# First batch's K loaded as fp32 on another queue, and half of the second batch's query transposes moved to TensorE

## The chip, the cores and the metric

The kernel runs on one core of one Trainium2 chip. The metric is device time in microseconds (us) of one execution. Traces are of single executions; where one execution differs from another by chance, the text says so.

## The reference

Linformer attention followed by a gated feed-forward layer. K and V are projected along the sequence by E and F (1024 to 64), then each query attends to 64 projected keys:

```python
k_proj = np.einsum('ks,bhsd->bhkd', E, k)        # E, F: 64 x 1024
v_proj = np.einsum('ks,bhsd->bhkd', F, v)
scores = scale * np.matmul(q, k_proj.transpose(0, 1, 3, 2))
attn = softmax(scores);  out = np.matmul(attn, v_proj)   # 8 batches, 8 heads, 1024 x 64
...
gate = 1.0 / (1.0 + np.exp(-(x @ w_gate)))       # x: 8192 x 512, d_ff 1536
return (gate * (x @ w_val)) @ w_out
```

## The kernel before

The feed-forward layer of one batch runs on TensorE while the attention of the next batch is slipped in between its matmuls. The first batch has nothing to hide behind: its K, Q and V must arrive, be projected and attended before the first feed-forward matmul. q, k, v and the weights are fp32 in memory and are cast to bf16 by the load, which the POOL queue issues. E and F go uncast on the SyncE queue. `busy(n)` issues n matmuls that compute nothing of use.

```python
def start_loads():
    for src, rows, n in ((E, slice(0, 64), "E"), (F, slice(64, 128), "F")):
        add("SP", lambda e, ...: e.dma_start(EF[rows, :], src[:, :]), ...)
    load_k(0)                     # POOL queue, casts to bf16
    ...                           # iota constants on POOL
    load_q_half(0, 0); load_v(0)
    ...
    load_w(0); load_w(1); load_q_half(0, 1); load_w(2); load_w(3)

def project_consts():             # 8 fp32 transposes of E and F, copied to EFT as bf16
    ...

start_loads()
constants()
project_consts()
busy(56)
bk = whole.next()
project(0, 0, [bk, bk], 0)        # K of batch 0: 16 bf16 matmuls of 256 columns
keep_k(bk, 0); turn_k(whole)
qt, sc, den, bc, xo = half_unit(0, whole)
qt(0); qt(1); sc(0); sc(1); den() # query transposes, scores, denominators
project(1, 1, bks, 0)             # V of batch 0
...                               # then the feed-forward loop; in it, for batch 1:
put(3, lambda: transpose_q(1))    # four DMA transposes of the queries
```

The softmax here doesn't subtract the row's maximum and nothing guards it: scores larger than these inputs give would overflow.

## Time and profile before

| | kernel before |
|---|---|
| time, median of 3 (range) | 580.94 us (580.69 to 581.57) |
| span of the profiled execution | 579.7 us |
| TensorE busy | 559.1 us, 96% |
| K, first half of Q, V of batch 0 landed | 12.65, 15.3, 20.4 us |
| unbroken feed-forward matmuls from | 25.81 us |
| from there to the end | 553.9 us |

### The profile page before, as it was taken

The numbers are of one execution on the slowest core, as the hardware profiler recorded it, in microseconds if no ns is written. First come the engines' busy times: TensorE is split into PE (matmuls) and PEld (weight loads), VectorE is DVE, ScalarE is ACT, GpSimd is POOL, SyncE is SP. The second block draws the span as 40 slices with busy tenths as digits, with TensorE's granted clock in tenths as the row PEclk, the third lists the DMA queues.
The fourth block names the chain that finished last, engine by engine and source line by source line (L and its number), as shares of the span: only waits on it lengthen the run. The fifth ranks groups of instructions, "written<-read, shape, count | busy, mean of one in ns | idle before, by whom it ended". The sixth has DMA issues, their size and how long they took to land.

```text
span 579.7 us, 7813 instructions
## 1 busy us (share of the span) xinstructions
PE 559.1 (96%) x3150; PEld 253.9 (44%) x3206; DVE 253.3 (44%) x393; ACT 201.0 (35%) x371; POOL 30.3 (5%) x43
## 2 busy tenths in 40 slices
PE   5799899999999999999999999999999999999997
PEld 4444334444454444444444444444445444444443
DVE  2355265345633636236442365434463363633332
ACT  1454541444233351343323433243423335222220
POOL 8100010100100000000100001000000000000000
PEclk9999999999999999999999999999999999999999
DMA  9999998963943049511586027650411001000012
GB/s 153 201 206 193 139 165 155 183 133 75 162 97 75 31 109 181 91 38 48 101 162 110 19 73 117 139 92 36 74 54 38 35 21 37 37 36 20 36 37 90
DMA packets 70756, 55.04 MB, mean 95 GB/s; under 512 B 31168, under 2 KB 62400, under 8 KB 70720
## 3 DMA queue, kind: packets, MB, share of 16 engines
q0 software_dynamic: 31776, 29.89, 33.5%
q1 hardware_dynamic: 38944, 24.65, 16.5%
q8 instruction: 25, 0.41, 0.3%
q14 instruction: 11, 0.09, 0.1%
HBM read 60.29 MB, written 16.78 MB: 133 GB/s over the span
## 4 chain that ended last, share of the span: by engine, by line
PE 85%; DMA 10%; POOL 2%; DVE 1%; issue 1%; SPq 0%; POOLq 0%; DVEq 0%
PE pF L216 77%; PE pA L216 8%; DMA Qb<-in_q_dram 5%; DMA qT<-Qb 5%; DVE rden L685 1%; POOL wV L234 1%; POOL wG L234 1%; POOL KV L234 0%; POOL Qb L234 0%; SPq L622 0%; DVE rhl L695 0%; DVE ost L826 0%; DVE hT L799 0%; DVE rhi L693 0%; POOL pat_i L298 0%
## 5 line engine op out<-in xcount | busy, mean ns | idle before, releaser
L799 DVE SCALAR_TENSOR_TENSOR hT<-sig,pF 128x512 bf16<-128x512 f32 x192 | 131.2, 686 | 210.0 <-PE pF L216 140.0
L220 ACT ACTIVATE sig<-pF 128x512 f32<-128x512 f32 x192 | 115.3, 601 | 273.6 <-PE pF L216 266.1
L216 PE MATMUL pF<-xT,wG 128*128 128x512 bf16 x749 | 195.4, 380 | 2.2 <-issue 1.4
L216 PE MATMUL pF<-xT,wV 128*128 128x512 bf16 x748 | 195.1, 379 | 1.9 <-DVE xT L604 0.9
L216 PE MATMUL pF<-wO,hT 128*128 128x512 bf16 x704 | 163.4, 379 | 1.6 <-issue 1.1
L216 PEld LDWEIGHTS pF<-xT,wV 128*128 128x128 bf16 x768 | 75.1, 98 | 90.8 <-issue 0.6
L216 PEld LDWEIGHTS pF<-xT,wG 128*128 128x128 bf16 x768 | 71.2, 98 | 94.0 <-issue 14.5
L216 PEld LDWEIGHTS pF<-wO,hT 128*128 128x128 bf16 x720 | 68.7, 98 | 86.4 <-issue 5.8
L826 DVE TENSOR_SCALAR ost<-pF 128x512 f32<-128x512 f32 x60 | 41.5, 691 | 89.1 <-PE pF L216 89.1
L220 ACT ACTIVATE rb<-pA 128x512 f32<-128x512 f32 x62 | 32.2, 606 | 26.6 <-PE pA L216 26.6
L220 ACT ACTIVATE eT<-pA 128x512 bf16<-128x512 f32 x63 | 32.8, 603 | 11.3 <-PE pA L216 11.3
L733 DVE TENSOR_TENSOR xT<-pA,rb 128x512 bf16<-128x512 f32 x56 | 34.6, 680 | 0.0
L685 DVE RECIPROCAL rden<-pA 128x128 f32<-128x128 f32 x28 | 23.7, 908 | 0.0
L234 POOL DMA_DIRECT2D KV<-in_k_dram x8 | 7.2, 904 | 265.7 <-PE pF L216 208.6
L216 PE MATMUL pA<-KV,EFT 128*64 128x256 bf16 x240 | 14.6, 274 | 0.9 <-DMA KV<-in_k_dram 0.9
L220 ACT ACTIVATE kp<-pA 128x256 bf16<-128x256 f32 x8 | 3.1, 383 | 35.9 <-PE pA L216 35.9
L216 PEld LDWEIGHTS pA<-KV,EFT 128*64 128x64 bf16 x240 | 12.5, 110 | 4.1 <-issue 3.0
L216 PE MATMUL pA<-qT,kpD 64*64 64x512 bf16 (+1 forms) x140 | 10.6, 367 | 2.1 <-DMA qT<-Qb 1.8
L234 POOL DMA_DIRECT2D KV<-in_v_dram x8 | 7.1, 885 | 80.2 <-PE pA L216 80.2
L220 ACT ACTIVATE vpD<-pA 64x256 bf16<-64x256 f32 x28 | 10.5, 375 | 0.5
L216 PE MATMUL pA<-wO,hT 128*128 128x512 bf16 x47 | 10.5, 379 | 0.1
L216 PE MATMUL pA<-eT,vpD 64*64 64x512 bf16 (+1 forms) x136 | 10.4, 370 | 0.0
(72 smaller groups left out, 113.1 us busy)
## 6 DMA issues: line engine op xcount, KB each, us to landing
out_dram<-ost SPq DMA_DIRECT2D x64, 256.0 KB, 2.0
KV<-in_k_dram POOLq DMA_DIRECT2D x8, 1024.0 KB, 10.1
KV<-in_v_dram POOLq DMA_DIRECT2D x8, 1024.0 KB, 13.2
Qb<-in_q_dram POOLq DMA_DIRECT2D x7, 1024.0 KB, 15.0
wO<-in_moe_w_out_dram POOLq DMA_DIRECT2D x1, 1536.0 KB, 50.2
Qb<-in_q_dram POOLq DMA_DIRECT2D x2, 512.0 KB, 16.5
wG<-in_moe_w_gate_dram POOLq DMA_DIRECT2D x2, 512.0 KB, 23.8
wV<-in_moe_w_val_dram POOLq DMA_DIRECT2D x2, 512.0 KB, 25.6
```

The costliest lines, as they stand in the source:

```text
L216: return add("PE", lambda e: e.matmul(o, lhsT, rhs, **kw), r=r, x=[("bank", b)])
L220: return add("ACT", lambda e: e.activation(o, i, func, scale=scale), r=r, w=w, x=x)
L234: add("POOL", lambda e: e.dma_start(o, i), r=r, w=w, dma=sem)
L685: lambda e, cc=cc: e.reciprocal(rden[:, cc], bank[bk][:, cc]),
L733: lambda e, r=r, g=g, n=n, bk=bks[g]: e.tensor_tensor(xT[s][:, r, :, 256 * g : 256 * g + 256], bank[bk][:, :].rearrange("p (f c) -> p f c" ...
L799: lambda e: e.scalar_tensor_tensor(hT[blk % 2][:, m, :], sg[:, :], 1.0, bank[pv][:, :], ALU.add, ALU.mult,),
L826: lambda e: e.tensor_scalar(o[:, :], bank[pb][:, :], 0.5, None, op0=ALU.mult),
```

## The change

The intent: get the first batch's K to TensorE sooner by not casting it and by using queues that are free at the start, and remove the wait for the last DMA transpose of the second batch's queries.

```diff
         for src, rows, n in ((E, ...), (F, ...)):
-                    "SP",
+                    "ACT",
                     lambda e, ...: e.dma_start(EF[rows, :], src[:, :]),
-            load_k(0)
+            for n in range(2):                        # K of batch 0, fp32, four heads each
+                add("SP", lambda e, n=n: e.dma_start(KF[n],
+                        k[0].rearrange("h (p t) d -> p h (t d)", t=NT)[:, 4*n : 4*n+4, :]), ...)
 ...
+        load_q_half(0, 0, r=["ident"]); load_v(0)     # now after all iotas
 ...
+                act(ETf[:, 4*g : 4*g+4, :], ... )     # fp32 copy of the turned E
 ...
         project_consts()
-        busy(56)
+        busy(6)
-        project(0, 0, [bk, bk], 0)
+        for n in range(2):                            # 2 x 16 fp32 matmuls of 128 columns
+            for t in range(NT):
+                for h in range(2):
+                    mm(bk, bank[bk][64*h : 64*h+64, P*n : P*n+P], ETf[:, t, :], kv4[:, h, t, :, :], ...)
 ...
-                put(3, lambda: transpose_q(1))
+                put(3, lambda: transpose_q(1, (2, 3)))
+                put(12, lambda: turn_q(1, 0))         # 8 TensorE transposes, one copy on VectorE
+                put(13, lambda: turn_q(1, 1))
```

The two fp32 halves of K lie in buffers that are not used yet (the second batch's turned queries, and the second buffer of attention outputs). The tile names in the profile therefore read `qT` and `xT`.

More of the change, by code (lines that the diff above doesn't have):

```diff
@@ L166, in bass_linformer_attn__then__ffn_glu_sigmoid_kernel @@
         EFT = sbuf("EFT", [P, NT, P], BF16)
+        ETf = sbuf("ETf", [P, NT, 64], FP32)
         Qb = [sbuf(f"Qb{i}", [P, H, S // P * DH], BF16) for i in range(2)]
@@ L265, in load_q, with load_q_half @@
             )
-        def load_q_half(b, hf):
+        def load_q_half(b, hf, r=()):
             s, cc = b % 2, slice(256 * hf, 256 * hf + 256)
@@ L273, in load_q_half @@
                 f"Q{s}{hf}",
+                r=r,
             )
@@ L281, in load_w @@
             load(wV[:, :, c], wv_v[:, :, c], [("wV", j)], f"wV{j}")
+        KA = qT[1][:, :, :].rearrange("p h c -> p (h c)").bitcast(FP32)
+        KB = xT[1][:, :, :, :].rearrange("p i f c -> p (i f c)").bitcast(FP32)
+        KF = [x.rearrange("p (h c) -> p h c", h=4) for x in (KA, KB)]
+        KFK = [[("qT", 1, r) for r in range(NR)], [("xT", 1, i, f, g) for i in range(NI) for f in range(2) for g in range(2)]]
         def start_loads():
@@ L291, in start_loads @@
                 )
-            load_k(0)
+            for n in range(2):
+                add(
+                    "SP",
+                    lambda e, n=n: e.dma_start(
+                        KF[n],
+                        k[0].rearrange("h (p t) d -> p h (t d)", t=NT)[:, 4 * n : 4 * n + 4, :],
+                    ),
+                    w=KFK[n],
+                    dma=f"KF{n}",
+                )
             pool(lambda e: e.iota(col_i[:, :], [[1, P]], channel_multiplier=0), w=["col_i"])
             pool(lambda e: e.iota(row_i[:, :], [[1, 1]], channel_multiplier=1), w=["row_i"])
-            load_q_half(0, 0)
-            load_v(0)
             pool(
@@ L309, in start_loads, with loads_q_v_w @@
             )
+        def loads_q_v_w():
+            load_q_half(0, 0, r=["ident"])
+            load_v(0)
             load_w(0)
@@ L407, in project_consts @@
             ev = EF[:, :].rearrange("k (p t) -> k t p", t=NT)
+            bs = []
             for g in range(2):
@@ L418, in project_consts @@
                     )
+                act(
+                    ETf[:, 4 * g : 4 * g + 4, :],
+                    bank[b][:, :].rearrange("p (t c) -> p t c", t=4)[:, :, 0:64],
+                    [],
+                    [("ETf", g)],
+                    b=b,
+                )
+                bs.append(b)
+            for g, b in enumerate(bs):
                 act(
@@ L615, in half_unit, with turn_q, transpose_q @@
             return qt, sc, den, bc, xo
-        def transpose_q(b):
+        def turn_q(b, r):
+            s, bk = b % 2, att.next()
+            ob = bank[bk][:, :].bitcast(BF16)
+            for h in range(2):
+                for t in range(4):
+                    c = 4 * h + t
+                    mm(
+                        bk,
+                        ob[:, c * P : (c + 1) * P],
+                        Qb[s][:, 2 * r + h, t * P : (t + 1) * P],
+                        ident[:, :],
+                        [("Q", s, 0), ("Q", s, 1), "ident"],
+                        tr=True,
+                    )
+            dve(
+                lambda e: e.tensor_copy(
+                    qT[s][:, 2 * r : 2 * r + 2, :].rearrange("p h c -> p (h c)"), ob[:, :]
+                ),
+                [],
+                [("qT", s, r)],
+                b=bk,
+            )
+        def transpose_q(b, rs=range(NR)):
             s = b % 2
-            for r in range(NR):
+            for r in rs:
                 add(
@@ L841, in bass_linformer_attn__then__ffn_glu_sigmoid_kernel @@
         constants()
+        loads_q_v_w()
         project_consts()
-        busy(56)
+        busy(6)
         bk = whole.next()
-        project(0, 0, [bk, bk], 0)
+        for n in range(2):
+            kv4 = KF[n].rearrange("p (r h) (t d) -> p h t r d", h=2, t=NT)
+            for t in range(NT):
+                for h in range(2):
+                    mm(
+                        bk,
+                        bank[bk][64 * h : 64 * h + 64, P * n : P * n + P],
+                        ETf[:, t, :],
+                        kv4[:, h, t, :, :],
+                        [("ETf", t // 4)] + KFK[n],
+                        start=(t == 0),
+                        stop=(t == NT - 1),
+                        tp=(0, 64 * h),
+                    )
         keep_k(bk, 0)
```

## The prediction

> **What bounds the kernel now.** I read the page first, then the timeline of the first 75 us, then the waits of TensorE, and the DMA issues of the first 16 us one by one. The page settles the large picture:
>
> ```profile
> span 579.7 us, 7813 instructions
> PE 559.1 (96%) x3150; PEld 253.9 (44%) x3206; DVE 253.3 (44%) x393; ACT 201.0 (35%) x371; POOL 30.3 (5%) x43
> PE   5799899999999999999999999999999999999997
> ```
>
> TensorE is busy nearly everywhere; only the first two slices (29 us) are thin. The waits of TensorE over the whole span say the same: beyond 2.5 us of issue gaps spread over the run, every wait of note is in the start, except one of 1.8 us:
>
> ```profile
> PE pA L216 <- DMA EF<-in_F_dram: 5.6, 1, 5.6
> PE pA L216 <- DMA qT<-Qb: 1.8, 1, 1.8
> PE pA L216 <- DMA KV<-in_k_dram: 0.9, 1, 0.9
> PE pF L216 <- DVE xT L604: 0.9, 1, 0.9
> PE pF L216 <- DMA Qb<-in_q_dram: 0.7, 1, 0.7
> PE pF L216 <- DMA KV<-in_v_dram: 0.6, 1, 0.6
> ```
>
> The columns are total, count and longest. So the change can only win in two places: the time before the dense feed-forward matmuls begin, and that one wait. TensorE's timeline shows both; columns are start, length, instruction group, and in brackets the idle time before it:
>
> ```profile
> 5.59 1.94 PE L216 MATMUL pA<-identf,EF 128*128 128x128 f32 x8 [5.59 <-DMA EF<-in_F_dram]
> 7.33 4.45 PE L216 MATMUL pF<-ident 128*128 128x128 bf16 x56
> 12.71 1.06 PE L216 MATMUL pA<-KV,EFT 128*64 128x256 bf16 x16 [0.94 <-DMA KV<-in_k_dram]
> 15.37 1.07 PE L216 MATMUL pF<-ident,Qb 128*128 128x128 bf16 x16 [0.68 <-DMA Qb<-in_q_dram]
> 20.48 1.06 PE L216 MATMUL pF<-KV,EFT 128*64 128x256 bf16 x16 [0.58 <-DMA KV<-in_v_dram]
> 25.30 0.38 PE L216 MATMUL pF<-xT,wV 128*128 128x512 bf16 x1 [0.86 <-DVE xT L604]
> ...
> 69.80 0.41 PE L216 MATMUL pA<-qT,kpD 64*64 64x512 bf16 x4
> 72.00 0.41 PE L216 MATMUL pA<-qT,kpD 64*64 64x512 bf16 x4 [1.79 <-DMA qT<-Qb]
> ```
>
> K, the first half of Q, and V each arrive a little after TensorE could take them; the 56 filler matmuls merely fill the wait for K. The dense part begins at 25.3 us. The last two lines are the second batch's scores, which wait for the last of four DMA transposes. The traffic behind these waits, by stage (the two numbers at the end are the DMA share and GB/s written to their destination):
>
> ```profile
> 2.00:4.00 2.00, 0.00 (x0) 0.00 (x0) 1.33 (x11) 0.02 (x1) 1.91 (x5) 1.00 0.80 227
> 4.00:10.00 6.00, 4.41 (x36) 4.37 (x37) 2.75 (x11) 1.19 (x2) 6.00 (x11) 1.00 0.99 142
> 10.00:25.00 15.00, 10.68 (x174) 7.62 (x172) 4.82 (x9) 6.80 (x13) 5.62 (x7) 1.00 1.36 201
> ```
>
> The casting loads write bf16, so 201 GB/s written is 402 GB/s read. From 4 to 10 us they run at only 142 (284 read), although DMA is never idle: some 0.35 MB, or 1.8 us at the later rate, is lost there.
>
> **What the Trainium skill says.** "DMA: Bandwidth & Descriptors", section "Issuing engines are not separate DMA queues": loads begun by the scalar, sync and gpsimd engines run on the same 16 DMA engines and interleave, so another queue saves only issue time. The trace before cannot refute it, but its two phases do differ: E and F from the SyncE queue reach 227 GB/s written in 2 to 4 us, the casting queue alone 142 after that. The section "SWDGE vs HWDGE vs iDMA" of the same page says that a cast needs the gpsimd path, which is why K must go as fp32 here. "FP8 and Floating Point Precision", section "TensorE Precision Notes": a true fp32 matmul takes four passes. The trace before has fp32 only as transposes (217 ns apart), so this is untested. "TensorE: Matmul & The Clock Gate", section "What's actually happening": TensorE runs at half rate until about 3.4 us of activity. The trace agrees: 12 of the filler matmuls begin in the microsecond from 8 us and 22 in that from 10 us, though the clock row of the page shows full speed.
>
> **The change part by part.**
>
> *K as fp32 on SyncE, E and F on ScalarE.* Removed: one casting load, issued at 1.25 and landed 11.4 us later, at 12.65. Added: two plain loads of 1 MB each, issued about 0.74 and 1.4 (where E and F stood before), with E and F beside them on ScalarE's queue. E and F landed 3.8 and 4.1 us after issue; sharing with K, I give them until about 6. Bytes read are unchanged (E and F 0.5 MB, K 2.1, half of Q 1.05, V 2.1 MB), bytes written for K double. At 400 GB/s E, F and K alone take 6.5 us from about 2.3, so 8.8; with the first Q and V packets in between I estimate 8 to 8.5 us for the first half of K and 11 (10 to 12) for the second.
>
> *Projection of K in fp32.* Before, 16 matmuls of 256 columns took 1.06 us: 53 ns apart, half of what 256 columns take alone (about 110 ns), so the two column halves run as pairs. After, 32 matmuls of 128 columns in four passes: a pair is 4 x 55 = 220 ns, eight pairs for a half of K 1.76 us, plus 0.16 tail, 1.9 us. The first half's share lies in the wait for the second half (even at the half rate 3.5 us, it would end near 12). On the path: 1.9 instead of 1.06.
>
> So: K landed 11.0, projected 12.95; then as before 0.5 us to the copy's end, 0.5 to the turned K, then the Q transposes (Q should be there by 12.5 instead of 15.3), which now begin at about 13.9 instead of 15.37. Scores follow at 15.4 instead of 16.86. That is 1.45 us sooner, and the chain to the V projection moves with it to 19.0, provided V lands by then.
>
> *V and everything behind it in the DMA stream.* V landed at 20.4. If the slow phase from 4 to 10 us is filled by K at the full rate, up to 2.5 us is won; if fp32 K is written at about 315 GB/s, it costs 6.7 us where its bf16 form needed 5.2 at 201, and about 1 us is left. I take 1.7: V at 18.7, just in time. The same shift applies to every later load, and they are tight: the third weight chunk landed at 33.5 for a matmul at 34.8, V of the second batch at 56.5 for 57.2, the output weights at 65.4 for 67.1. A start of the dense part sooner by more than the stream's shift plus these slacks would meet new waits. The gain at the start: 1.4 us.
>
> *Small parts.* Two more copies on ScalarE (128x256 took 0.38 us each) before the fp32 K matmuls lie within the wait for K. 50 fillers fewer cost nothing, if TensorE is otherwise busy enough to reach full rate.
>
> *Half of the transposes on TensorE.* Added: 16 transposes of 128x128; the same 16 for the second half of the first batch occupy 0.89 us of the dense part (30.86 to 31.75). Two copies of 0.69 us on VectorE, which is 44% busy, lie beside the matmuls. Removed: two of four DMA transposes. They landed 12.2, 10.0, 11.7 and 3.0 us after issue, the last at 71.86; the two that stay should be down near 66 minus the shift, for scores at about 70. So the wait of 1.79 us goes: net 0.9 us won.
>
> Sum: 1.4 + 0.9 = 2.3 us, from 580.94 to about 578.6.
>
> **The rivals.** *First*, the DMA engines are the limit of the start: K comes sooner, but Q and V, pushed back by K's doubled writes, end the wait instead. For it: DMA is busy throughout the start, and bytes read are the same. Against it: the poor rate from 4 to 10 us. Then only the 0.9 us is won: 580. *Second*, the fp32 projection costs more than K's earlier landing wins: if column halves do not pair in fp32, the second half takes 3.6 us, the start gains nothing or loses 0.3; also 580 to 580.5; with a cold TensorE (gaps with few fillers) it might be 582. *Third*, the plain loads are far better than I think and K is down by 9.5 and V by 17.5: then the start is 2.5 to 3 us sooner, and the time 577 or a little less. *Fourth*, a shifted TensorE runs into the second batch's V or the output weights and gives back up to 1 us.
>
> **Range and chances.** The sum lies between 0 (rivals one or two, and new waits) and 5 us, hence 576.0 to 580.8. Two per cent would be 11.6 us, more than the whole start could yield, and a loss of that size has no cause that I can see: within 2% is nearly sure.
>
> **What would show it.** Right: the second half of K landing at 10 to 12 us, its matmuls 1.7 to 1.9 us long; V's projection near 19 and the first feed-forward matmul near 23.9; no wait for a DMA transpose at the second batch's scores, and 16 more transposes costing 0.9 us around 53 us. Wrong: fp32 matmuls of a half taking over 3 us; V landing at 20 or later; a new wait on weights, V or the output weights between 30 and 67 us; or TensorE at half rate after 12 us.

## More of the kernel before

The 32 executions of the kernel before that ran beside the experiments lie between 579.83 and 582.72 us, so differences of a few tenths of a microsecond are read from traces, not from times.

The record also gives each execution's mean granted clock, the share of full speed at which TensorE was allowed to run.

After 25.81 us TensorE starts a full-width matmul every 0.22 us. So the span is the start plus the dense part, and each part of the change can be judged on its own term.

## The result, and the profile after

The changed kernel takes 583.48 us (median of 4, 583.15 to 583.92) against 581.01 us (median of 4) of the kernel before. The ratio is 1.0042, with a 95% interval of 1.0025 to 1.0059. Ratios here are the mean time of one kernel's runs over that of the other's in the same rounds, so they are not quite the ratio of the medians quoted. Executions over 1.5% slower than the fastest of the same kernel are left out of the means. It is 2.5 us slower: within 2%, as expected, but outside the predicted range and on the other side.

The page of the changed kernel, the waits of TensorE (total, count, longest), and its timeline:

```profile
span 581.7 us, 7900 instructions
PE 565.1 (97%) x3220; PEld 255.0 (44%) x3220; DVE 254.6 (44%) x395; ACT 201.5 (35%) x373; POOL 29.4 (5%) x42
PE   3899999999999999999999999999999999999997
```

```profile
PE pA L217 <- DMA EF<-in_F_dram: 9.5, 1, 9.5
PE pA L217 <- DVE rhl L746: 1.0, 1, 1.0
```

```profile
9.53 1.95 PE L217 MATMUL pA<-identf,EF 128*128 128x128 f32 x8 [9.53 <-DMA EF<-in_F_dram]
11.27 0.84 PE L217 MATMUL pF<-ident 128*128 128x128 bf16 x6
12.04 3.33 PE L217 MATMUL pA<-qT,ETf 128*64 128x128 f32 x32
15.21 1.91 PE L217 MATMUL pA<-xT,ETf 128*64 128x128 f32 x32
17.98 1.07 PE L217 MATMUL pF<-ident,Qb 128*128 128x128 bf16 x16
22.44 1.06 PE L217 MATMUL pF<-KV,EFT 128*64 128x256 bf16 x16
28.31 0.39 PE L217 MATMUL pF<-xT,wG 128*128 128x512 bf16 x1
...
69.94 0.63 PE L217 MATMUL pA<-qT,kpD 64*64 64x512 bf16 x8
70.50 2.77 PE L217 MATMUL pF<-wO,hT 128*128 128x512 bf16 x12
73.19 0.63 PE L217 MATMUL pA<-qT,kpD 64*64 64x512 bf16 x8
```

The waits for K, Q and V are all gone, and yet the dense part starts 2.5 us later (28.31 instead of 25.81). One wait has taken their place: TensorE does nothing at all until F lands at 9.4 us, where before it began at 5.59. It then works without a pause to 17.1 us on what should have been hidden. The eight transposes take 1.95 us. The first half of the K projection takes 3.33 us, most of it before the array reaches full rate: the second half, with the same work, takes 1.91. (Each fp32 matmul leaves two records, hence x32.) The clock records stored in the trace (times from which a granted clock held) agree: the first one, to full speed, comes at 14.88 us, against 9.74 in the kernel before, whose fillers go from 107 to 56 ns apart at that moment. At the end of the extract, the scores of the second batch wait for nothing. The dense part is 581.7 - 28.31 = 553.4 us, only 0.5 less than before.

The traffic of the changed kernel by stage (last number: GB/s written; the same stages of the kernel before are in the prediction), then the queues from 2.3 to 12.6 us, of the kernel before and of the changed one:

```profile
2.00:4.00 2.00, 0.00 (x0) 0.00 (x0) 2.00 (x15) 1.24 (x1) 1.61 (x2) 1.00 0.72 213
4.00:10.00 6.00, 0.47 (x3) 0.51 (x4) 1.13 (x4) 0.00 (x0) 6.00 (x9) 1.00 1.07 271
```

```profile
q0 software_dynamic: 1541, 1.31, 87.9%
q1 hardware_dynamic: 159, 0.52, 18.8%
```

```profile
q1 hardware_dynamic: 1013, 2.03, 68.1%
q10 hardware_dynamic: 160, 0.52, 19.6%
q0 software_dynamic: 484, 0.25, 17.3%
```

The second number is MB written. A casting load (the queue named software) reads twice what it writes, so in these 10.3 us the kernel before read 2 x 1.31 + 0.52 = 3.14 MB and the changed one 2.03 + 0.52 + 2 x 0.25 = 3.05 MB: 305 and 296 GB/s. More is written, nothing more is read. The landings follow (the last number is us from issue):

```profile
qT<-in_k_dram SPq DMA_DIRECT2D x1, 1024.0 KB, 8.4
xT<-in_k_dram SPq DMA_DIRECT2D x1, 1024.0 KB, 12.0
EF<-in_E_dram ACTq DMA_DIRECT2D x1, 256.0 KB, 6.3
EF<-in_F_dram ACTq DMA_DIRECT2D x1, 256.0 KB, 8.1
```

Issued at 0.74 and 1.26, the halves of K landed at 9.1 and 13.3, the second later than the whole bf16 K before (12.65). F was issued at 1.32 and landed at 9.4. V landed at 19.7 instead of 20.4 (issue at 3.39 plus 16.3), but by the second batch's Q nothing of that was left: 43.9 instead of 43.6.

### The profile page after: what moved, and what is told of

It reads as the page before. It is cut to its first block, busy times and chain, and to the rows that moved or that the text cites. A ratio compares the mean times of both kernels' runs of the same rounds, so it can differ in the third digit from the quotient of the medians.

```text
span 581.7 us, 7900 instructions
## 1 busy us (share of the span) xinstructions
PE 565.1 (97%) x3220; PEld 255.0 (44%) x3220; DVE 254.6 (44%) x395; ACT 201.5 (35%) x373; POOL 29.4 (5%) x42
## 4 chain that ended last, share of the span: by engine, by line
PE 95%; DVE 2%; DMA 1%; ACT 1%; issue 0%; ACTq 0%; DVEq 0%
PE pF L217 85%; PE pA L217 11%; DMA EF<-in_F_dram 1%; DVE rden L736 1%; ACT eT L221 0%; DVE xT L632 0%; ACT qT L221 0%; DVE rden L579 0%; DVE vpD L490 0%; DVE rhl L746 0%; DVE ost L877 0%; DVE hT L850 0%; ACTq L295 0%; DVE rhi L744 0%; ACT kp L221 0%
## 5 line engine op out<-in xcount | busy, mean ns | idle before, releaser
L217 PE MATMUL pF<-xT,wG 128*128 128x512 bf16 x768 | 198.7, 380 | 0.6 <-ACT rb L221 0.3
L217 PE MATMUL pF<-xT,wV 128*128 128x512 bf16 x768 | 198.2, 379 | 0.2 <-DVE xT L632 0.2
L217 PE MATMUL pF<-wO,hT 128*128 128x512 bf16 x720 | 165.4, 380 | 0.0
L217 PE MATMUL pA<-identf,EF 128*128 128x128 f32 x8 | 1.9, 422 | 9.5 <-DMA EF<-in_F_dram 9.5
L221 ACT ACTIVATE vpD<-pA 64x256 bf16<-64x256 f32 x28 | 10.5, 375 | 0.5
```

What stands on the lines that cost most here:

```text
L217: return add("PE", lambda e: e.matmul(o, lhsT, rhs, **kw), r=r, x=[("bank", b)])
L221: return add("ACT", lambda e: e.activation(o, i, func, scale=scale), r=r, w=w, x=x)
```

## The experiments

Twelve runs, in four sets of runs sharing their executions of the kernel before (medians 580.98 to 581.16 us). The theory after reading the trace was that the late landing of E and F pushed everything (A), with a TensorE still at half rate as a rival (B). Other letters are explained in the expectations. "Start" is the first of the unbroken feed-forward matmuls, "rest" the span minus it.

| run | time, us (median) | ratio to before, 95% | start | rest |
|---|---|---|---|---|
| before | 580.94 | | 25.81 | 553.9 |
| changed | 583.48 | 1.0042 (1.0025 to 1.0059) | 28.31 | 553.4 |
| ef_first | 583.78 | 1.0049 (1.0029 to 1.0069) | 28.73 | 553.4 |
| prewarm | 582.02 | 1.0015 (0.9994 to 1.0035) | 25.68 | 553.3 |
| k_only | 582.43 | 1.0022 (1.0002 to 1.0043) | 28.50 | 552.4 |
| turn_only | 581.61 | 1.0011 (0.9991 to 1.0031) | 26.80 | 553.3 |
| ef_on_act | 580.56, one run | none | 25.87 | 552.7 |
| ef_first_warm | 583.49 | 1.0047 (1.0027 to 1.0068) | 27.61 | 553.3 |
| q_held | 584.56 | 1.0070 (1.0051 to 1.0089) | 26.97 | 553.3 |
| q_held_act | 583.66 | 1.0046 (1.0026 to 1.0066) | 29.20 | 553.3 |
| before_warm | 580.14 | 0.9988 (0.9973 to 1.0003) | 26.59 | 552.4 |
| turn_warm | 581.10 | 1.0022 (0.9990 to 1.0055) | 26.06 | 553.3 |
| prewarm_k_only | 580.29 | 0.9990 (0.9978 to 1.0002) | 26.63 | 552.5 |
| before_warm_again | 580.00 | 0.9988 (0.9972 to 1.0004) | 28.26 | 552.4 |

Start and rest are of the one profiled execution; the times are of all. The start varies by a microsecond or so between executions of one kernel. The rest is 553.3 or 553.4 in every trace with transposes on TensorE; with four DMA transposes it lies between 552.4 and 553.9.

### ef_first: E and F ahead of K on SyncE

```diff
-                    "ACT",
+                    "SP",          # E and F, issued before the two halves of K
```

> The changed kernel with E and F moved back to the SyncE queue, ahead of the two K halves. Theory A (E and F landed 4 us late, at 9.4 us, because their packets shared the DMA engines with K, and everything behind them slid): F lands at 5.5 to 6 us, the first half of K near 9, the second half near 13.3 as before; the K projection then ends 1.9 us after the second half, near 15.3 instead of 17.1, and the dense part begins 1.8 us sooner than in the changed kernel (near 26.5), time about 581.6. Rival B (the fp32 projection and the cold clock are the cost, not the landing of E and F): the K projection still ends at 16.5 or later and the time stays near 583.

Measured: F landed in time, at 5.5 us, and nothing was won (583.78 us).

```profile
5.54 1.94 PE L217 MATMUL pA<-identf,EF 128*128 128x128 f32 x8 [5.54 <-DMA EF<-in_F_dram]
7.28 0.84 PE L217 MATMUL pF<-ident 128*128 128x128 bf16 x6
10.71 3.68 PE L217 MATMUL pA<-qT,ETf 128*64 128x128 f32 x32 [2.58 <-DMA qT<-in_k_dram]
14.92 2.62 PE L217 MATMUL pA<-xT,ETf 128*64 128x128 f32 x32 [0.53 <-DMA xT<-in_k_dram]
```

The wait has moved: now it is for K, whose halves came 1.5 us later (issued behind E and F, at 2.00 and 2.63), and TensorE is still slow when they arrive, because six fillers do not bridge 2.6 us. Theory A alone falls.

### prewarm: fillers before E and F

```diff
+        busy(80)
         project_consts()
         busy(6)
```

> The changed kernel with 80 filler matmuls on TensorE ahead of the transposes of E and F, so that TensorE is at full rate when they land. Theory B (cold TensorE): transposes of E and F take about 1.1 us instead of 1.95, the first half of the K projection about 1.9 instead of 3.3; both halves end at about 15 instead of 17.1, dense part about 2 us sooner, time about 581.5. Theory A alone with the clock without weight: nothing changes, the projection ends at 17 and the time stays 583.5.

Measured: 582.02 us, 1.5 us under the changed kernel, and in the trace the start is at 25.68.

```profile
2.14 6.26 PE L217 MATMUL pF<-ident 128*128 128x128 bf16 x80 [2.14 <-DVE half L347]
8.78 1.14 PE L217 MATMUL pA<-identf,EF 128*128 128x128 f32 x8 [0.38 <-DMA EF<-in_F_dram]
9.75 0.50 PE L217 MATMUL pF<-ident 128*128 128x128 bf16 x6
10.18 1.97 PE L217 MATMUL pA<-qT,ETf 128*64 128x128 f32 x32
12.52 1.97 PE L217 MATMUL pA<-xT,ETf 128*64 128x128 f32 x32 [0.38 <-DMA xT<-in_k_dram]
```

E and F still land late (8.6 us in this execution, 0.8 sooner than in the changed kernel's), but the transposes take 1.14 instead of 1.95 us and the first half of K 1.97 instead of 3.33. That half now lies before the second half's landing, as the prediction had it. Theory B holds: all four executions of prewarm (581.03 to 582.75 us) lie under all four of the changed kernel (583.15 and up), though the two intervals in the table overlap. The profiled execution is the fastest of its four, so its start of 25.68 is on the lucky side. In the kernel before, the fillers, meant as idle work behind the transposes, had been doing the warming.

### k_only and turn_only: the two parts apart

```diff
 k_only:     changed kernel, put(3, lambda: transpose_q(1)), no turn_q
 turn_only:  kernel before,  put(3, lambda: transpose_q(1, (2, 3))), turn_q at 12 and 13
```

> The changed kernel with all four DMA transposes of the second batch's queries, none on TensorE. Theory C (the late start had already swallowed the wait of 1.8 us for the last DMA transpose, so the transposes on TensorE are a pure cost of 0.9 us here): no wait over 0.3 us for a DMA transpose at the second batch's scores, and the time is 0.5 to 0.9 us under the changed kernel, near 582.8. Rival D (the wait is still there without them): a wait of 1 to 1.8 us before the last scores and a time 0.5 to 1 us over the changed kernel.

> The kernel before with only the second part of the change: half of the second batch's queries transposed by TensorE. From the prediction's sum: 1.8 us of wait gone, 0.9 us of transposes added, so 580.1. Theory E (about 0.5 us comes back as a longer wait for the reciprocals' split, as the changed kernel's trace shows 0.95 us there instead of 0.43): net 0.3 to 0.4 us won, near 580.6, which the time alone will hardly show and the trace will.

Measured: k_only 582.43 us, about 1 us under the changed kernel, its rest 552.4 us instead of 553.4. All four DMA transposes landed in time, since TensorE arrived later while the loads did not. The last of the four was also issued sooner, at 67.7 us; in the profiled execution of the kernel before it was 68.8, in the four other profiled executions with four of them 66.9 to 67.7, so the wait of 1.8 us was at the long end. So theory C holds: there the TensorE transposes remove a wait that the late start has already removed, and cost 1.0 us. turn_only: no difference in time (581.61 us); its rest is 553.3 us, 0.6 less than the kernel before. Part of the wait of 1.8 us comes back a few microseconds later, as theory E has it. The lines are of the kernel before and of turn_only:

```profile
79.65 0.39 PE L216 MATMUL pA<-rhl,bsel 32*128 32x512 bf16 x4 [0.43 <-DVE rhl L695]
```

```profile
80.07 0.40 PE L216 MATMUL pA<-rhl,bsel 32*128 32x512 bf16 x4 [0.95 <-DVE rhl L718]
```

The start of turn_only was late, 26.80, by chance of that execution: full speed came early (8.49 us), so its fillers ended at 11.2, TensorE waited 1.48 us for K, and then its clock fell back: the trace records 0.50 from 15.3 to 22.1 us. The Q transposes took 1.89 us instead of 1.07.

### ef_on_act: is the ScalarE queue slow of itself?

```diff
 kernel before:
-                    "SP",
+                    "ACT",         # E and F only; K stays a casting load
```

> The kernel before with only E and F moved to the ScalarE queue, K still the casting load. Theory A1 (E and F landed at 9.4 us in the changed kernel because K's plain loads on SyncE took the engines beside them): here F lands at 5 to 6 us, as before, and the start is that of the kernel before. Rival A2 (the ScalarE queue itself is slow, behind the activation table load or otherwise): F lands at 8 us or later here too.

Measured: one run, 580.56 us. F landed at 6.2 us, 4.9 after issue:

```profile
EF<-in_F_dram ACTq DMA_DIRECT2D x1, 256.0 KB, 4.9
```

So the queue is not slow, A1 holds: beside K's plain loads the same transfer took 8.1 us. The wait for the last DMA transpose was 0.6 us in this execution, not 1.8.

### ef_first_warm, q_held and q_held_act: which load gates a warm start

```diff
 ef_first_warm: ef_first, with busy(40) before project_consts()
 q_held:        ef_first_warm, with load_q_half(0, 0, r=["ident"] + KFK[0])   # Q waits for K's first half
 q_held_act:    q_held with E and F on "ACT" again, busy(44)
```

> The changed kernel with E and F first on SyncE and 40 fillers ahead of their transposes. Theory F (with TensorE warm the landing of the second half of K is the gate, and loads of Q and V beside K set it): K's second half lands near 14.7 as in the run with E and F first, its projection ends 2.0 us later near 16.8, the dense part begins near 27.4 and the time is near 582.8, no better than with E and F on ScalarE and a warm TensorE (582.0). Rival: K lands by 13 and the dense part begins at 25.5 or sooner.

> As the run before, with the loads of Q, V and all weights held until the first half of K has landed. Theory F: E, F and K have the DMA engines to themselves, 2.6 MB at about 400 GB/s, so the second half of K lands at 9.5 to 10.5 instead of 14.7, and its projection ends near 12.3; Q lands near 13, V near 19, dense part near 24 to 25, time 579.5 to 581. Rival (the plain loads are slow of themselves): K's second half lands at 12.5 or later.

> As the run with Q held, but with E and F on the ScalarE queue beside K, as the change has it, and TensorE warmed. Theory F: second half of K at 9 to 10 us, F at 6.5 to 8 (it shares with K alone), dense part near 24 to 25, time 579.5 to 581.

Measured: ef_first_warm 583.49 us, its second K half landing near 14.4 and projected in 1.97 us, as expected. While TensorE waited 2.51 us for the first half its clock fell back (0.50 from 9.8 to 13.2 us), and that half took 3.36 us. q_held was a miss. With E, F and K alone on the DMA engines the second half still landed at 11.5 us, 8.9 after its issue at 2.63, not at 9.5 to 10.5:

```profile
qT<-in_k_dram SPq DMA_DIRECT2D x1, 1024.0 KB, 6.9
xT<-in_k_dram SPq DMA_DIRECT2D x1, 1024.0 KB, 8.9
EF<-in_F_dram SPq DMA_DIRECT2D x1, 256.0 KB, 4.1
```

That is 2.62 MB between 2.3 and 11.5 us, 285 GB/s. Meanwhile Q and V, issued only at 9.57 and 10.57, became the waits (1.1 and 1.2 us), and the clock fell to 0.50 from 17.0 to 20.4 us. The profiled execution, 582.32 us, is the fastest of five; why the others took 584.4 to 585.5 no trace shows. q_held_act likewise missed (583.66 us): F landed 7.5 us after issue although no load of Q or V was in flight, so K's plain loads alone delay it; its 44 fillers ended 2.9 us before F, and the transposes took 1.94 us again. Here the clock column (third from the end) shows it, but for the equally slow transposes of the changed kernel it shows full speed. The first line is of q_held_act, the second of the changed kernel:

```profile
10.00:11.00 1.00, 1.00 (x8) 0.93 (x7) 0.00 (x0) 0.41 (x2) 1.00 (x2) 0.50 0.75 264
```

```profile
10.00:11.00 1.00, 1.00 (x6) 1.00 (x5) 0.00 (x0) 0.35 (x1) 1.00 (x2) 1.00 1.18 313
```

The column counts the time before a trace's first clock record, 14.88 us in the changed kernel, as full speed. So a TensorE that has not yet been warm is seen in the spacing of its matmuls alone. In the twelve profiled executions in which TensorE worked without a break up to that first record, it came 2.8 to 6.0 us after TensorE's first matmul (turn_only and ef_on_act): how many fillers are enough differs from execution to execution.

### before_warm and turn_warm: can warming help the kernel before?

```diff
+        busy(16)
         project_consts()
-        busy(56)
+        busy(92)
```

> The kernel before with 16 fillers ahead of the transposes of E and F and 92 instead of 56 behind them, nothing else. Theory G (the clock gate costs the kernel before about 1 us in some executions, as the profiled execution of the run with TensorE transposes alone shows with its cold Q transposes of 1.89 us): time 0.2 to 0.8 us under the kernel before, mean granted clock 0.999 or 1.0 in all executions. Rival: the fillers make no difference, 581.0, or run past the landing of K and cost up to 0.5 us.

> The same fillers with half of the second batch's queries transposed by TensorE, the only part of the change that wins when the dense part starts on time. From the trace (dense part 553.3 us with it, 553.9 us without): 0.5 to 0.6 us under the run with fillers alone, 580.2 to 580.6. Rival: within noise of it, because the wait for the last DMA transpose varies from execution to execution (1.8 us and 0.6 us were seen).

Measured: 580.14 us with fillers alone, 0.8 us lower, interval up to 1.0003; the clock in all four executions was 0.999 or 1.0. Of the 32 executions of the kernel before, 15 had a clock of 0.997 or less; they took 581.36 us on average, the other 17 took 580.75. That fits theory G, but does not show it: before_warm's profiled start, 26.59, is no sooner. turn_warm came out at 581.10 us, not below it (one of its four took 584.50, at a clock of 0.991): its rest is 553.3 us, while before_warm's DMA transposes landed in time in the profiled execution and its rest is 552.4. The expectation of a gain of 0.5 us missed; of the rival, the reason holds (the wait varies), but the result is about 1 us slower, not the same.

### prewarm_k_only and before_warm_again

```diff
 prewarm_k_only: prewarm, with put(3, lambda: transpose_q(1)), no turn_q
```

> The changed kernel with TensorE warmed by 80 fillers and with all four DMA transposes, that is the first part of the change with its cold start repaired and without the second part. From the sums of the traces: dense part from 25.7 us as in the run with fillers, 552.4 to 553.9 us long according to the wait for the last DMA transpose, so a span of 578.1 to 579.6 and a time of 580.0 to 581.4: the same as the kernel before, 0.5 to 1 us under the run with fillers and TensorE transposes (582.0). If the time is 582 or more, the K part has another cost that the traces have not shown.

> The kernel before with the fillers, again, with more rounds, since it came out 0.1% under the kernel before with an interval that touches 1. If the cold spells of some executions are real, again 0.5 to 1 us under, interval below 1. Rival: 581.0, the first result was luck.

Measured: prewarm_k_only 580.29 us, ratio 0.9990: the whole loss of the changed kernel is gone. It was profiled in an execution where F landed at 9.7 us, and still:

```profile
9.87 1.14 PE L217 MATMUL pA<-identf,EF 128*128 128x128 f32 x8 [0.47 <-DMA EF<-in_F_dram]
11.27 1.97 PE L217 MATMUL pA<-qT,ETf 128*64 128x128 f32 x32
13.48 1.97 PE L217 MATMUL pA<-xT,ETf 128*64 128x128 f32 x32 [0.24 <-DMA xT<-in_k_dram]
```

The start is 26.63 there, against 28.31 of the changed kernel with F at 9.4. before_warm_again: median 580.00, but two of six executions took 582.35 and 582.49, and the interval touches 1 again. The profiled one of these shows the price of a fixed number of fillers: F landed late at 7.0, the 92 fillers then ran to 16.0 us, though K had been there since 12.4. The other had a clock of 0.994 and no trace. No version beats the kernel before clearly; prewarm_k_only and before_warm beat the changed kernel.

## Why the prediction was wrong

**What bounds the kernel.** Right: the time is the start plus a dense part, which lies between 552.4 and 553.9 us in every trace.

**The step that failed first: the warm TensorE.** The prediction said "50 fillers fewer cost nothing, if TensorE is otherwise busy enough to reach full rate", and that the first half of the fp32 projection "lies in the wait for the second half". It had the condition from the Trainium skill, "TensorE: Matmul & The Clock Gate", section "What's actually happening" (about 3.4 us of activity), and did not check it against its own late E and F. Without fillers before 9.5 us TensorE was idle, so the transposes and most of K's first half ran at the low rate, on the path. The projection took 5.1 us of the path instead of 1.9. Removing only this (prewarm against changed, prewarm_k_only against k_only) gives back 1.5 and 2.1 us of the 2.5. What was missing is work before 9.5 us, not the 50 fillers as such: behind the transposes they could only have begun at 11.3, when K's first half had landed. No run put them back there.

**Mis-sized terms behind it.** The projection was to end at 12.95 us and ended at 17.1. By an estimate from the trace, 1.9 us of that is the low rate (13.3 plus 1.97 would be 15.2), and 2.3 us the later landing of K's second half. E and F "until about 6": 9.4 in the changed kernel, 6.2 on the same queue without K's plain loads. K's second half at 11: 13.3. Both rest on "at 400 GB/s". The prediction blamed the slow phase from 4 to 10 us on the casting queue and let plain loads fill it; the same 10.3 us moved 305 GB/s read before and 296 after, and K with E and F alone got 285. V at 18.7: 19.7, and the shift of 1.7 for later loads was nil. So even warm the change only ties: the start of prewarm is that of the kernel before within the scatter. That is the first rival's outcome, DMA as the limit of the start, though K itself came no sooner either (its second half at 12.5 us in prewarm, all of K at 12.65 before). V, down at 20.0 us in prewarm, was just in time for its matmuls at 20.01 and would have held up an earlier K. The remark in the second rival on a cold TensorE, set at 582, is what happened.

**The fp32 matmuls.** Right: 1.97 us for a half once warm, against 1.9. The column halves do pair: in prewarm two records start 7 ns apart and the next two 109 ns later.

**The transposes.** Their cost was right (16 more took 0.9 us), the net gain of 0.9 was not. Against a wait of 1.8 us it is 0.6, since 0.5 us of the wait reappears before the broadcast of the reciprocals (0.43 to 0.95; the sum would leave 0.4, and 0.2 us is not accounted for). Against no wait it is a loss of 0.9: rest 553.3 with TensorE transposes in all traces, and 552.4 without them when the DMA transposes are in time. In the changed kernel the late start had removed the wait, and in other executions it was 0.6 or absent. One trace was taken for all.

**What stays open.** Why reads average near 300 GB/s in the first ten microseconds and 402 later, whichever queue issues most of them, no run tells. The average hides more: q_held moved 334 to 399 GB/s in each microsecond from 6 to 10, but 131 from 4 to 5. Why one execution's loads land half a microsecond to one and a half sooner or later than another's, neither.

## What to carry to other kernels

Before fillers are removed, ask what else keeps TensorE busy before the first real work: an array that sits idle until a small transfer lands pays twice for it, in the wait and in slow matmuls after it. Another queue added no read bandwidth at the start here, and a small transfer that everything needs should not be issued beside a large one. A wait seen in one trace is worth removing only if it is there in other executions too, and only its part that does not reappear at the next dependency.

## What the Trainium skill lacked or had wrong

- "DMA: Bandwidth & Descriptors", section "Issuing engines are not separate DMA queues", held: the same bytes were read in the same time from other queues. It lacks a figure for how a small transfer fares beside a large one: F, 256 KB behind E on ScalarE's queue, took 8.1 us beside K's plain loads and 4.9 beside K's casting load.
- The same page has no figure for the first microseconds of a kernel: about 300 GB/s were read from 2.3 to 12.6 us, and 402 from 10 to 25 us in the kernel before.
- "TensorE: Matmul & The Clock Gate", section "What's actually happening", held in kind: equal halves of work took 3.33 and 1.91 us. But full rate came 2.8 to 6.0 us after the first matmul. No page says that the profile's clock row counts the time before the first clock record as full speed, so that a first low rate must be read from the spacing of matmuls (107 and 56 ns).
- The same page, section "Part 4: PE-mode transpose", says that the full rate doesn't engage for transposes. Here transposes ran at it once TensorE was warm: the eight fp32 ones took 1.95 us cold and 1.14 warm, and 16 bf16 ones between matmuls 0.89 us. Whether transposes alone would warm TensorE, no run tells.
- "FP8 and Floating Point Precision", section "TensorE Precision Notes", held: 16 fp32 matmuls of 128 columns took 1.97 us, and 218 ns for each of eight pairs is four times the 55 ns of one pass. No page says that column halves still pair in fp32.
